# Attention and two MoE layers on one core: even heads with raw fp32 probabilities and V, bias pieces and Q's low parts on VectorE

## The chip, the core and the metric

The kernel runs on one core of a Trainium2 chip. Five engines take their instructions in order, each from its own queue: TensorE (PE; its weight loads are shown apart as PEld), VectorE (DVE), ScalarE (ACT), GpSimd (POOL) and SyncE (SP, which issues DMAs). They wait for each other through semaphores. The metric is the device time of one execution in microseconds.

## What is computed

Attention over 2 batches, 8 heads, 576 positions and 64 channels with a bias that a small network makes of the relative position, then two mixture-of-experts layers with 8 experts each. The change is in attention alone:

```python
scores = scale * np.matmul(q, k.transpose(0, 1, 3, 2))
x = (psi_rel / psi_i)[..., None]            # 576 x 576, from log1p of distance and position
h = np.maximum(x @ w1 + b1, 0.0)            # 32 hidden
bias = h @ w2                               # one column a head
scores = scores + bias.transpose(2, 0, 1)[None, :, :, :]
scores = scores - np.max(scores, axis=-1, keepdims=True)
attn = np.exp(scores)
attn = attn / (np.sum(attn, axis=-1, keepdims=True) + 1e-09)
return np.matmul(attn, v).astype(np.float32)
```

## The kernel before

Queries are cut into nine tiles `t` of 128 rows: tiles 0 to 7 are four row blocks `it` of both batches in turn, tile 8 holds the last 64 rows of both batches. A tile has 8 heads, so there are 72 pairs (t, h), walked in this order.

The bias does not depend on the batch. It is made per row block `it` in pieces of 32 keys (`NPC` is 18; the last block has 9 pieces, since its two batches share them). Each piece is one comparison on DVE (`bias_mask`, tile `mask`, L246 or L249), 16 matmuls into one PSUM bank (`bias_mm`, tile `pm`, L259) and `bias_out`: either ACT copies `pm` out (`abst`, L271) and POOL multiplies and adds (`btmp`, L272; `bias`, L273), or, with `direct`, DVE does both steps from PSUM (L267, L268). Before, only pieces 5, 9 and 13 of block 0 are direct. Block 0 is made ahead of the first head, the blocks 1 to 4 between the heads of the block before. In the heads `pm` has a single buffer, `mask` three and `btmp` two.

For a head, `s_mm` makes scores of two fp32r parts of Q (L321), `s_max` adds the bias and takes the maximum on DVE (L329), `s_exp` is the exponential on ACT with the row sum (L339), `p_turn` transposes four blocks of 128 keys on PE into PSUM (L353). `p_hi` has ACT write the transposed probabilities, times 4096, as f16 (`pth`, L359), `p_lo` has DVE write what f16 left out (`ptl`, L364), and `av` multiplies them with V in three f16 matmuls for each of the four blocks: high by high, high by low, low by high (L382). V has its f16 parts `VH` and `VL` from `v_split` (L302, L303), after its largest magnitude has been found (`v_sums`, `v_scale`). 576 is 4 x 128 + 64: the remainders of two heads at a time share a block, so a tile has a ninth product `h == H` with the remainder's V (`VRH`, `VRL`, L310, L311). `recip` (L388 to L390) and `finish` (L396) divide by the sums.

`s_mm` runs `LEAD` (3) heads ahead and `s_exp` one; `av` of a head stands two heads behind. Q is split into fp32r parts by ACT and POOL (`q_split`, L152, L153), once a tile; K by ACT and DVE (L167). The code order is a wish only: a scheduler places the instructions of attention on the engines by its own costs; the last eight steps of tile 8 stand in an order written by hand (`manual_schedule`). The MoE layers behind begin with what `finish` wrote.

The lines of `av` that count:

```python
for i, (l_, r_) in enumerate(((th, vh), (th, vl), (tl, vh))):
    nc.tensor.matmul(o.acc[ii, cs], l_[:, cc, ii], r_, start=h == 0 and cc == 0 and i == 0, stop=i == 2,
```

Of the kernel before, what the change touches and what calls it, by code (L numbers as in the profile page):

```python
# [95 lines left out]
def attention(tc, ctx, g, a, out, setup, on_tile, on_slot):  # L96
# [89 lines left out]
    vraw = prep.tile([P, BH * 4 * D], F32, name="vraw")  # L186
    for x in range(2):
        nc.sync.dma_start(vraw[:, x * 2 * VC:(x + 1) * 2 * VC], a["a_v"][:, x * 2 * VC:(x + 1) * 2 * VC])
    vrem = prep.tile([P, BH // 2, D], F32, name="vrem")
    nc.sync.dma_start(vrem, a["a_vr"].rearrange("p (t d) -> p t d", d=D))  # L190
# [89 lines left out]
    def v_sums(vm, x):  # L280

        junk = prep.tile([P, VC], F16, tag="junk", name="junk", bufs=2)
        src = vraw[:, x * VC:(x + 1) * VC] if x < 4 else vrem.rearrange("p a d -> p (a d)")
        nc.scalar.activation(junk[:, :src.shape[1]], src, AF.Abs, accum_out=vm[:, x:x + 1])

    def v_scale(vm, stage_):
        if stage_ == 0:
# [9 lines left out]
        return pow2_scales(nc, keep, vmx, "sv")  # L297

    def v_split(x):
        cs = slice(x * VC, (x + 1) * VC)  # L300
        vh = VH.rearrange("p a b d -> p (a b d)")[:, cs]
        nc.scalar.mul(vh, vraw[:, cs], sv)  # L302
        nc.vector.scalar_tensor_tensor(VL.rearrange("p a b d -> p (a b d)")[:, cs], vraw[:, cs], sv, vh, ALU.mult, ALU.subtract)  # L303

    def v_rem():
        nc.gpsimd.memset(VRH, 0.0)
        nc.gpsimd.memset(VRL, 0.0)
        for r in range(2):
            rr = slice(r * 64, r * 64 + 64)
            nc.scalar.mul(VRH[rr, :, r], vrem[rr], sv[rr])  # L310
            nc.vector.scalar_tensor_tensor(VRL[rr, :, r], vrem[rr], sv[rr], VRH[rr, :, r], ALU.mult, ALU.subtract)  # L311
# [43 lines left out]
    def p_hi(t, h, ccs=slice(0, 4)):  # L355
        o = tiles[t]
        if h not in o.av:
            o.av[h] = [late.tile([P, 4, P], F16, tag=f"pt{x}", name="pt" + x, bufs=5) for x in "hl"]
        nc.scalar.mul(o.av[h][0][:, ccs], o.pt[h][:, ccs], PSC)  # L359

    def p_lo(t, h, ccs=slice(0, 4)):
# [915 lines left out]
```

## Time and profile before

| what | value |
|---|---|
| three runs, median (lowest to highest) | 645.55 us (643.68 to 645.91) |
| profiled execution, its own time | 643.15 us |
| span of the profiled execution | 641.4 us |
| busy share PE, DVE, ACT, POOL | 85%, 73%, 62%, 50% |
| granted clock of PE, mean | 0.962 |

Attention takes the first 253 us of the span, the two MoE layers the rest. Ahead of the heads, until about 53 us, stand the bias of block 0 and the preparation of Q, K and V. A busy share of the whole span says little here, as the stretches have different limits. In the rows below times are in us from the span's start unless marked ns. Instructions of one engine overlap a little at their ends, so prices of one are read from start to start where a row of the next is given; a matmul's duration holds its whole way through the array, of which only a small part keeps the next one waiting.

### The profile page before, as it was taken

Reading aid. Unit: us, or ns where it says so; the run is one execution under the profiler, and the core shown is the slowest. Engines: PE = TensorE matmul, PEld = TensorE weight load, DVE = VectorE, ACT = ScalarE, POOL = GpSimd, SP = SyncE. Lnnn points to the kernel's source line nnn. Section 1 sums busy time; section 2 is a strip of 40 time slices with the busy share of each in tenths; the row PEclk is TensorE's granted clock in tenths of the full one; section 3 lists DMA queues with packets and bytes.
Section 4 is the critical chain, followed back from the end, with each engine's and each line's share of the span. In section 5 each row is a group of like instructions: output and inputs, shape, how many; then the busy total and the mean of one; then the engine's idle time right before and its main releaser. Section 6 shows DMA issues by size and latency. Waiting matters only on the chain. (4 is left out here: it accounts for less than half of the span.)

```text
span 641.4 us, 13184 instructions
## 1 busy us (share of the span) xinstructions
PE 546.4 (85%) x4970; PEld 461.5 (72%) x4970; DVE 466.1 (73%) x721; ACT 399.8 (62%) x667; POOL 319.4 (50%) x285
## 2 busy tenths in 40 slices
PE   2455678888888999789999999999889999999991
PEld 2444667778887888567788788777767887877771
DVE  5799999999999786887951262189768924948960
ACT  3566877888888865567842452378516736837840
POOL 3997899988877460425431141144213422434440
PEclk9777979998999999999999999999899999999997
DMA  7921654111010492788980180078755932957900
GB/s 222 326 77 34 164 136 138 49 51 28 19 35 19 85 306 69 220 264 296 330 304 29 59 276 30 30 249 292 258 165 167 330 129 84 322 171 216 336 5 8
DMA packets 47909, 101.44 MB, mean 158 GB/s; under 512 B 11780, under 2 KB 13700, under 8 KB 47536
## 3 DMA queue, kind: packets, MB, share of 16 engines
q1 hardware_dynamic: 40640, 92.12, 44.8%
q0 software_dynamic: 6272, 7.49, 3.6%
q8 instruction: 63, 1.03, 0.7%
q14 instruction: 54, 0.44, 0.2%
q10 hardware_dynamic: 880, 0.35, 0.2%
HBM read 97.47 MB, written 13.67 MB: 173 GB/s over the span
## 5 line engine op out<-in xcount | busy, mean ns | idle before, releaser
L911 DVE TENSOR_TENSOR wl<-raw,wh 128x1024 fp32r<-128x1024 f32 x125 | 156.4, 1289 | 20.8 <-ACT wh L898 15.7
L964 PE MATMUL py<-wh,hT 128*128 128x512 f32 x400 | 141.2, 404 | 0.0
L898 ACT CAST wh<-raw 128x1024 fp32r<-128x1024 f32 x110 | 113.9, 1051 | 6.5 <-ACTq L1169 2.6
L994 DVE TENSOR_TENSOR hT<-pt,hT 128x512 fp32r<-128x512 f32 x50 | 34.6, 692 | 89.0 <-ACT hT L993 88.9
L272 POOL TENSOR_TENSOR btmp<-abst,xp 128x256 f32<-128x256 f32 x78 | 80.1, 1027 | 17.1 <-ACT abst L271 16.0
L964 PEld LDWEIGHTS py<-wh,hT 128*128 128x128 f32 x400 | 75.2, 188 | 15.1
L259 PE MATMUL pm<-wmov,mask 128*128 128x64 f16 x1296 | 58.8, 204 | 29.8 <-DVE wmov L234 12.3
L964 PE MATMUL py<-wl,hT 128*128 128x512 f32 x200 | 78.2, 391 | 0.0
L259 PEld LDWEIGHTS <-mask 128*128 128x128 f16 x1296 | 53.0, 106 | 34.6 <-DVE mask L246 24.5
L273 POOL TENSOR_TENSOR bias<-abst,btmp 128x256 f32<-128x256 f32 x78 | 72.1, 925 | 5.8
L321 PE MATMUL s<-K,Q 128*128 128x288 f32 x320 | 63.3, 322 | 12.7 <-DVE mx L329 9.5
L339 ACT ACTIVATE P<-sb,mx 128x576 f32<-128x576 f32 x72 | 55.8, 776 | 24.4 <-DVE mx L329 20.3
L246 DVE TENSOR_TENSOR mask<-toep,T 128x1024 f16<-128x1024 f16 x72 | 70.3, 993 | 0.8 <-PE pm L259 0.5
L271 ACT ACTIVATE abst<-pm,swi 128x512 f32<-128x512 f32 x78 | 53.0, 685 | 20.1 <-PE pm L259 18.6
L353 PE MATMUL pt<-ident,P 128*128 128x128 f32 x324 | 54.2, 290 | 10.1 <-DVE ptl L364 5.7
L329 DVE CUSTOM_DVE_ANT_0 sb<-s,bias 128x576 f32<-128x576 f32 x72 | 53.9, 751 | 7.9 <-PE s L321 4.5
L364 DVE SCALAR_TENSOR_TENSOR ptl<-pt,pth 128x512 f16<-128x512 f32 x81 | 54.8, 680 | 5.2 <-ACT pth L359 5.0
L964 PE MATMUL ph<-wh,xh 128*128 128x512 f32 x120 | 50.1, 418 | 8.6 <-PEq L1169 7.7
L321 PEld LDWEIGHTS s<-K,Q 128*128 128x128 f32 x320 | 46.8, 194 | 14.0 <-issue 8.4
L359 ACT ACTIVATE pth<-pt 128x512 f16<-128x512 f32 x81 | 47.6, 592 | 8.6 <-PE pt L353 7.3
L993 ACT CAST hT<-pt 128x512 fp32r<-128x512 f32 x50 | 29.4, 587 | 36.4 <-PE pt L988 31.8
L1033 POOL DMA_INDIRECT y_tok<-y,si x13 | 18.0, 1382 | 67.6 <-ACT y L1025 41.1
(216 smaller groups left out, 1189.7 us busy)
## 6 DMA issues: line engine op xcount, KB each, us to landing
raw<-m_w_dram SPq DMA_DIRECT2D x64, 512.0 KB, 5.1
...
```

The lines of the kernel that those rows point to most:

```text
L246: nc.vector.tensor_tensor(m, w, T[:, i0:i0 + P].unsqueeze(1).to_broadcast([P, 8, P]), ALU.is_gt)
L259: nc.tensor.matmul(pm[:, :, :, gq * 4:gq * 4 + 4], m[:, gq], wmov[:, part], start=part == 0, stop=part == 1)
L272: nc.gpsimd.tensor_tensor(tmp, ab_[:, 0], xp, ALU.mult)
L273: nc.gpsimd.tensor_tensor(biases[it][:, :, cs], ab_[:, 1], tmp, ALU.add)
L321: nc.tensor.matmul(ps[:, half, :288], Q[:, part, h], K[:, b * H + h, half * 288:half * 288 + 288], start=i == 0, stop=i == last)
L329: nc.vector.tensor_tensor_reduce(sb.rearrange("p (t j) -> p t j", t=2), o.ps.pop(h)[:, :, :288], biases[o.it][:, h].rearrange("p (t j) -> ...
L339: nc.scalar.activation(o.Pt[hp][:, x * S:(x + 1) * S], sb, AF.Exp, bias=mx, scale=-1.0, accum_out=o.sums[:, h:h + 1])
L353: nc.tensor.transpose(pt[:, cc], src, ident)
L364: nc.vector.scalar_tensor_tensor(tl[:, ccs], o.pt.pop(h)[:, ccs], PSC, th[:, ccs], ALU.mult, ALU.subtract)
L898: eng.copy(hi, r)
L911: eng.tensor_tensor(lo, self.raw.pop((ge, j)), hi.bitcast(F32), ALU.subtract)
L964: self.nc.tensor.matmul(ps, x[a_][:, xs], w[b_][:, ws], start=first and i == 0, stop=last and i == 2)
```

## The change

- Even heads (`whole(h)`) keep V as it is (`V_`, fp32) and the transposed probabilities as fp32 (`pT`, one copy by ACT); `av` has one fp32 matmul per block in place of three f16 ones, and `p_lo` does nothing for them. Odd heads stay as they were. The remainder product also is fp32: half of its rows, of the odd heads, are scaled to fit (`VR`, `odd`). In the hand-written end two of the copies are DVE's.
- Only the odd heads' V is split: two `v_sums` and two `v_split` remain of five and four; `v_rem` goes.
- In block 0 eight pieces are direct instead of three; in the later blocks every third piece (`w[1] % 3 == 1`), 21 in all.
- Q's low parts are DVE's for all tiles but the first.
- Buffers: `pT` three; `pth` and `ptl` two each instead of five; `mx` three instead of four.

```diff
-VC = BH * 4 * D // 4
-VAT = 11, 13, 15, 17
-DIRECT = 5, 9, 13
+DIRECT = 1, 3, 5, 7, 9, 11, 13, 15
...
-    VH = keep.tile([P, BH, 4, D], F16, name="VH")
-    VL = keep.tile([P, BH, 4, D], F16, name="VL")
-    VRH = keep.tile([P, BH // 2, 2, D], F16, name="VRH")
-    VRL = keep.tile([P, BH // 2, 2, D], F16, name="VRL")
+    V_ = keep.tile([P, BH // 2, 4, D], F32, name="V")
+    VR = keep.tile([P, BH // 2, 2, D], F32, name="VR")
+    VH = keep.tile([P, BH // 2, 4, D], F16, name="VH")
+    VL = keep.tile([P, BH // 2, 4, D], F16, name="VL")
+    odd = keep.tile([P, 2], F32, name="odd")
...
-            nc.gpsimd.tensor_tensor(Q[:, 1], qr, Q[:, 0].bitcast(F32), ALU.subtract)
+            (nc.vector if t else nc.gpsimd).tensor_tensor(Q[:, 1], qr, Q[:, 0].bitcast(F32), ALU.subtract)
...
+        sv, isv = pow2_scales(nc, keep, vmx, "sv")
+        nc.vector.tensor_scalar(odd[:, 0:1], sv, PSC, None, ALU.mult)
+        nc.vector.tensor_scalar(odd[:, 1:2], isv, 1 / PSC, None, ALU.mult)
+        nc.vector.tensor_scalar(VR[64:, :, 1], VR[64:, :, 1], odd[64:, 0:1], None, ALU.mult)
+        return sv
...
-        mx = late.tile([P, 1], F32, tag="mx", name="mx", bufs=4)
+        mx = late.tile([P, 1], F32, tag="mx", name="mx", bufs=3)
...
+    def whole(h):
+        return h % 2 == 0
+
+    def p_out(t, h, eng=nc.scalar):
...
+        if whole(h):
+            o.av[h] = late.tile([P, 4, P], F32, tag="pT", name="pT", bufs=3)
+            (eng.copy if eng is nc.scalar else eng.tensor_copy)(o.av[h], o.pt.pop(h))
+        else:
+            o.av[h] = [late.tile([P, 4, P], F16, tag=f"pt{x}", name="pt" + x, bufs=2) for x in "hl"]
+            nc.scalar.mul(o.av[h][0], o.pt[h], PSC)
...
-        th, tl = o.av[h]
-        nc.vector.scalar_tensor_tensor(tl[:, ccs], o.pt.pop(h)[:, ccs], PSC, th[:, ccs], ALU.mult, ALU.subtract)
...
+        if not whole(h):
+            th, tl = o.av[h]
+            nc.vector.scalar_tensor_tensor(tl, o.pt.pop(h), PSC, th, ALU.mult, ALU.subtract)
...
+                if h == H:
+                    terms = [(pT, VR[:, b * 4 + cc].rearrange("p t d -> p (t d)"))]
+                elif whole(h):
+                    terms = [(pT, V_[:, (b * H + h) // 2, cc])]
                 else:
...
+                    vh, vl = VH[:, (b * H + h) // 2, cc], VL[:, (b * H + h) // 2, cc]
+                    terms = [(pT[0], vh), (pT[0], vl), (pT[1], vh)]
...
-            bias_out(*w)
+            bias_out(*w, w[1] % 3 == 1)
         outq = []
         p_turn(*u)
-        p_hi(*u)
+        p_out(*u)
...
-        p_hi(t, 6)
-        p_lo(t, 6)
+        p_out(t, 6, nc.vector)
...
-        p_hi(t, H)
+        p_out(t, H, nc.vector)
```

DVE at the end of the part ahead of the heads, before (`btmp` and `bias` with `pm` are the two steps of a direct piece, `sb,mx` is the first L329):

```order
L246 TENSOR_TENSOR mask<-toep,T 128x1024
L268 SCALAR_TENSOR_TENSOR bias<-pm,swi,btmp 128x8x32
L303 SCALAR_TENSOR_TENSOR VL<-vraw,svs,VH 128x1024 x3
L311 SCALAR_TENSOR_TENSOR VRL<-vrem,svs,VRH 64x8x64 x2
L303 SCALAR_TENSOR_TENSOR VL<-vraw,svs,VH 128x1024
L661 COPY enT<-pt 128x32
L329 ISA sb,mx<-s,bias 128x576
```

The same place on DVE after:

```order
L247 TENSOR_TENSOR mask<-toep,T 128x1024 x2
L268 SCALAR_TENSOR_TENSOR btmp<-pm,swi,xp 128x256
L247 TENSOR_TENSOR mask<-toep,T 128x1024
L269 SCALAR_TENSOR_TENSOR bias<-pm,swi,btmp 128x8x32
L307 SCALAR_TENSOR_TENSOR VL<-vraw,svs,VH 128x1024
L247 TENSOR_TENSOR mask<-toep,T 128x1024
L268 SCALAR_TENSOR_TENSOR btmp<-pm,swi,xp 128x256
L247 TENSOR_TENSOR mask<-toep,T 128x1024
L269 SCALAR_TENSOR_TENSOR bias<-pm,swi,btmp 128x8x32
L661 COPY enT<-pt 128x32
L247 TENSOR_TENSOR mask<-toep,T 128x1024
L325 ISA sb,mx<-s,bias 128x576
```

The splits of V that stood in a row are fewer and spread, direct pieces alternate with masks up to the first head, and two masks of block 1 (the last two here) now stand ahead of it.

DVE early in tile 1, behind `finish` of tile 0, before:

```order
L396 TENSOR_TENSOR x<-acc,rinv 128x512
L246 TENSOR_TENSOR mask<-toep,T 128x1024
L364 SCALAR_TENSOR_TENSOR ptl<-pt,pth 128x512
L329 ISA sb,mx<-s,bias 128x576
L329 ISA mx 128x1
L167 TENSOR_TENSOR K<-kraw,K 64x1152
L364 SCALAR_TENSOR_TENSOR ptl<-pt,pth 128x512
L246 TENSOR_TENSOR mask<-toep,T 128x1024
L329 ISA sb,mx<-s,bias 128x576
```

And after:

```order
L402 TENSOR_TENSOR x<-acc,rinv 128x512
L268 SCALAR_TENSOR_TENSOR btmp<-pm,swi,xp 128x256
L247 TENSOR_TENSOR mask<-toep,T 128x1024
L269 SCALAR_TENSOR_TENSOR bias<-pm,swi,btmp 128x8x32
L325 ISA sb,mx<-s,bias 128x576
L325 ISA mx 128x1
L166 TENSOR_TENSOR K<-kraw,K 64x1152
L247 TENSOR_TENSOR mask<-toep,T 128x1024
L152 TENSOR_TENSOR Q<-qraw,Q 128x1024
L368 SCALAR_TENSOR_TENSOR ptl<-pt,pth 128x512
L325 ISA sb,mx<-s,bias 128x576
```

Where each head had its `ptl`, one of two is left; a direct piece's two steps, with a mask between them, and Q's subtraction stand in the queue instead.

## Rows read from the trace of the kernel before

**Rows 1.** Busy time by stretch: from:to, length, busy time and count per engine, PE clock, DMA.

```profile
40.00:54.00 14.00, 4.06 (x45) 3.53 (x46) 13.36 (x18) 9.21 (x12) 13.45 (x10) 0.61 0.33 85
120.00:140.00 20.00, 17.54 (x313) 16.07 (x312) 20.00 (x38) 16.70 (x36) 18.93 (x19) 1.00 0.14 42
220.00:235.00 15.00, 14.86 (x187) 13.89 (x187) 12.96 (x32) 11.61 (x28) 5.81 (x4) 1.00 0.84 244
```

**Rows 2.** Timeline of POOL ahead of the heads: start, duration, instruction.

```profile
51.18 1.58 POOL L273 TENSOR_TENSOR bias<-abst,btmp 128x256 f32<-128x256 f32 x1
```

**Rows 3.** Timeline of DVE ahead of the heads; in brackets idle time and releaser.

```profile
26.48 0.48 DVE L267 SCALAR_TENSOR_TENSOR btmp<-pm,swi,xp 128x256 f32<-128x256 f32 x1 [2.90 <-POOL bias L273]
...
43.55 4.70 DVE L303 SCALAR_TENSOR_TENSOR VL<-vraw,svs,VH 128x1024 f16<-128x1024 f32 x3
48.18 2.34 DVE L311 SCALAR_TENSOR_TENSOR VRL<-vrem,svs,VRH 64x512 f16<-64x512 f32 x2
...
52.80 0.76 DVE L329 CUSTOM_DVE_ANT_0 sb<-s,bias 128x576 f32<-128x576 f32 x1 [0.51 <-POOL bias L273]
```

**Rows 4.** Groups of DVE's instructions, 54.16 to 250 us: count, busy us, mean ns, idle before.

```profile
L246 DVE TENSOR_TENSOR mask<-toep,T 128x1024 f16<-128x1024 f16 x53 | 53.8, 1023 | 0.2
L364 DVE SCALAR_TENSOR_TENSOR ptl<-pt,pth 128x512 f16<-128x512 f32 x79 | 53.5, 680 | 5.2 <-ACT pth L359 5.0
...
L167 DVE TENSOR_TENSOR K<-kraw,K 64x1152 fp32r<-64x1152 f32 x6 | 10.9, 1816 | 0.2
...
L388 DVE TENSOR_SCALAR rinv<-sums 128x8 f32<-128x8 f32 x8 | 5.8, 720 | 0.3 <-ACT P L339 0.3
```

**Rows 5.** Timeline of DVE and POOL in tile 1.

```profile
101.33 0.69 DVE L246 TENSOR_TENSOR mask<-toep,T 128x1024 f16<-128x1024 f16 x1
101.94 0.67 DVE L364 SCALAR_TENSOR_TENSOR ptl<-pt,pth 128x512 f16<-128x512 f32 x1
102.53 0.74 DVE L329 CUSTOM_DVE_ANT_0 sb<-s,bias 128x576 f32<-128x576 f32 x1
...
106.07 2.38 POOL L153 TENSOR_TENSOR Q<-qraw,Q 128x1024 fp32r<-128x1024 f32 x1
...
106.84 2.17 DVE L246 TENSOR_TENSOR mask<-toep,T 128x1024 f16<-128x1024 f16 x1
```

**Rows 6.** Line L167: shortest, median, longest ns, first and last start.

```profile
L167 DVE TENSOR_TENSOR K<-kraw,K x8: 1355/1642/3414, 20.7 to 96.6; 64x1152 fp32r<-64x1152 f32 x8
```

**Rows 7.** Timeline of DVE near attention's end.

```profile
250.22 0.16 DVE L388 TENSOR_SCALAR rinv<-sums 128x8 f32<-128x8 f32 x1
```

**Rows 8.** Timeline of PE in tile 1.

```profile
101.46 1.06 PE L692 MATMUL s<-enT,xT 128*128 128x8 f32 x8 [1.31 <-DVE mx L329]
...
103.09 0.19 PE L382 MATMUL acc<-VH,pth 128*128 128x64 f16 x1
...
103.44 0.63 PE L353 MATMUL pt<-ident,P 128*128 128x128 f32 x4
103.83 0.78 PE L321 MATMUL s<-K,Q 128*128 128x288 f32 x4
104.44 0.64 PE L259 MATMUL pm<-wmov,mask 128*128 128x64 f16 x16
```

**Rows 9.** Timeline of PE, the remainder's product and what follows.

```profile
239.18 0.22 PE L382 MATMUL acc<-VRH,pth 128*128 128x128 f16 x1
...
239.85 0.61 PE L353 MATMUL pt<-ident,P 128*128 128x128 f32 x4
```

**Rows 10.** Timeline of DVE, the last step of tiles 1 and 5.

```profile
118.56 0.68 DVE L396 TENSOR_TENSOR x<-acc,rinv 128x512 f32<-128x512 f32 x1
...
205.71 0.68 DVE L396 TENSOR_TENSOR x<-acc,rinv 128x512 f32<-128x512 f32 x1
```

**Rows 11.** Timeline of PE, scores of two heads of tile 8.

```profile
230.29 1.30 PE L321 MATMUL s<-K,Q 128*128 128x288 f32 x8
...
232.18 1.30 PE L321 MATMUL s<-K,Q 128*128 128x288 f32 x8
```

More of the change, by code (lines that the diff above doesn't have):

```diff
@@ L185, in attention @@
     k_load(0)
[L186 to L190, printed above, removed]
+    vraw = prep.tile([P, BH // 2, 4, D], F32, name="vraw")
+    for v, half in ((vraw, 1), (V_, 0)):
+        nc.sync.dma_start(v.rearrange("p a c d -> p (a c d)"), a["a_v"][:, half * BH * 2 * D:(half + 1) * BH * 2 * D])
+    nc.gpsimd.memset(VR, 0.0)
+    for r in range(2):
+        rr = slice(r * 64, r * 64 + 64)
+        nc.sync.dma_start(VR[rr, :, r], a["a_vr"][rr].rearrange("p (t d) -> p t d", d=D))
     k_load(1)
@@ L296, in v_scale, with v_split @@
         nc.vector.tensor_copy(vmx, v_scale.p[:, P:P + 1])
[L297 to L311, printed above, removed]
+        sv, isv = pow2_scales(nc, keep, vmx, "sv")
[3 more added lines that the diff above has]
+        return sv
+    def v_split(b):
+        raw = vraw[:, b * 4:b * 4 + 4].rearrange("p a c d -> p a (c d)")
+        vh, vl = (x[:, b * 4:b * 4 + 4].rearrange("p a c d -> p a (c d)") for x in (VH, VL))
+        nc.scalar.mul(vh, raw, sv)
+        nc.vector.scalar_tensor_tensor(vl, raw, sv, vh, ALU.mult, ALU.subtract)
     def s_mm(t, h):
@@ L353, in p_turn, with p_lo, av @@
             nc.tensor.transpose(pt[:, cc], src, ident)
-    def p_hi(t, h, ccs=slice(0, 4)):
+    def whole(h):
+        return h % 2 == 0
+    def p_out(t, h, eng=nc.scalar):
         o = tiles[t]
[L357 to L361, printed above, removed]
+        if whole(h):
[4 more added lines that the diff above has]
+            nc.scalar.mul(o.av[h][0], o.pt[h], PSC)
+    def p_lo(t, h):
         o = tiles[t]
-        th, tl = o.av[h]
-        nc.vector.scalar_tensor_tensor(tl[:, ccs], o.pt.pop(h)[:, ccs], PSC, th[:, ccs], ALU.mult, ALU.subtract)
-    def av(t, h, ccs=range(4)):
+        if not whole(h):
+            th, tl = o.av[h]
+            nc.vector.scalar_tensor_tensor(tl, o.pt.pop(h), PSC, th, ALU.mult, ALU.subtract)
+    def av(t, h):
         o = tiles[t]
@@ L369, in av @@
             o.acc = psA.tile([P, 512], F32, tag="acc", name="acc")
-        th, tl = o.av[h]
-        for cc in ccs:
+        pT = o.av.pop(h)
+        for cc in range(4):
             for b, _, _ in o.qs:
@@ L374, in av @@
                 pos = None if t < 8 else (0, b * 64)
-                if h < H:
-                    cs = slice(h * D, (h + 1) * D)
-                    vh, vl = VH[:, b * H + h, cc], VL[:, b * H + h, cc]
-                else:
-                    cs = slice(cc * P, (cc + 1) * P)
-                    vh, vl = (V_[:, b * 4 + cc].rearrange("p t d -> p (t d)") for V_ in (VRH, VRL))
-                for i, (l_, r_) in enumerate(((th, vh), (th, vl), (tl, vh))):
-                    nc.tensor.matmul(o.acc[ii, cs], l_[:, cc, ii], r_, start=h == 0 and cc == 0 and i == 0, stop=i == 2,
+                cs = slice(h * D, (h + 1) * D) if h < H else slice(cc * P, (cc + 1) * P)
+                if h == H:
+                    terms = [(pT, VR[:, b * 4 + cc].rearrange("p t d -> p (t d)"))]
+                elif whole(h):
+                    terms = [(pT, V_[:, (b * H + h) // 2, cc])]
+                else:
+                    vh, vl = VH[:, (b * H + h) // 2, cc], VL[:, (b * H + h) // 2, cc]
+                    terms = [(pT[0], vh), (pT[0], vl), (pT[1], vh)]
+                for i, (l_, r_) in enumerate(terms):
+                    nc.tensor.matmul(o.acc[ii, cs], l_[:, cc, ii], r_, start=h == 0 and cc == 0 and i == 0, stop=i == len(terms) - 1,
                                      tile_position=pos, skip_group_check=True)
@@ L387, in recip @@
         r = o.r = bw.tile([P, H], F32, tag="rinv", name="rinv")
-        nc.vector.tensor_scalar(r, o.sums, 1e-9, PSC, ALU.add, ALU.mult)
+        nc.vector.tensor_scalar(r, o.sums, 1e-9, None, ALU.add)
         nc.vector.reciprocal(r, r)
-        nc.vector.tensor_scalar(r, r, isv, None, ALU.mult)
+        nc.vector.tensor_scalar(r[:, 1::2], r[:, 1::2], odd[:, 1:2], None, ALU.mult)
     def finish(t):
@@ L403, in attention @@
     rot = (psM, "pm"), (psT, "pt"), (psT, "pt"), (psS, "s"), (psS, "s")
-    vm = prep.tile([P, 6], F32, name="vm")
+    vm = prep.tile([P, 4], F32, name="vm")
     for x in range(NPC + 2):
```

44 lines of the change are left out of this document (19 added, 25 removed).

## The prediction

> **What bounds the kernel now.** I read the stretches first [rows 1]. In the middle of attention VectorE (DVE) is busy 20.00 of 20 us while TensorE (PE) shows 17.54, and PE's figure is inflated, since its instructions overlap. So DVE sets the pace of the heads. Towards the end of attention (220 to 235 us) the masks are gone and PE is busy 14.86 of 15: there PE sets it. Ahead of the heads GpSimd (POOL) does, 13.45 of 14 us in 40 to 54 [rows 1]: its bias additions follow each other to 52.76 [rows 2], and the first subtraction of scores on DVE (L329, at 52.80) waits its last 0.51 us for them [rows 3]. The MoE layers behind take their input from attention's end and none of their code changes, so I let them move with it.
>
> DVE's own rows then say what its time is made of [rows 4]. A mask takes 1023 ns in the mean, but 0.69 us where nothing disturbs it; where POOL subtracts the low parts of Q (2.38 us from 106.07) the mask that starts at 106.84 takes 2.17 us and ends with POOL [rows 5]. The two engines shut each other out. The evictions `ptl` that read PSUM are not touched: 680 ns in the mean, 0.67 us beside POOL's work too [rows 4, 5]. Nor is a bias step from PSUM: 0.48 us [rows 3]. The Trainium skill's SBUF — State Buffer (Who interferes with whom) says the same of a DVE instruction with two SBUF inputs: it and a GpSimd instruction that reads SBUF hold one port for the whole instruction. By that rule the Q subtraction on DVE stays exposed to POOL, with which the price of K's subtraction below agrees.
>
> **Ahead of the heads** (to the first L329). POOL loses 5 of its 15 pieces, a third of its chain, and is no longer last. With it go DVE's waits for POOL, 2.90 and 0.51 us: -3.4. DVE drops two of four `VL` splits (three take 4.70, so 1.57 each): -3.1, and both `VRL` (2.34): -2.3 [rows 3]. It takes five more pieces of two steps, each 0.48 less the 0.07 by which DVE instructions overlap, 0.82 a piece: +4.1 [rows 3]. Scaling half of VR and two one-column products: no such row; between 0.3 and the 1.17 of one VRL step, I take 0.8 in all. Masks: 14 follow here, each some 0.2 over its floor by the heads' rows below once Q's collisions are left out; with a third of POOL's pieces gone I take a third of that: -1.0. Sum -4.9. New is that DVE, which takes its queue in order, waits for PE's 16 matmuls of its own pieces; behind it stand masks, for which PE waits in turn. The schedule puts a mask between, so I take 0.6 for all eight, between 0 and 4. **-4.3** (bounds -6 and -1). The two masks of the next block that now stand ahead of the first L329 are only moved.
>
> **The heads as far as DVE sets the pace** (54 to 215). Prices from start to start, as instructions overlap by about 0.07.
> - `ptl` of even heads and remainders goes: 45 of 81. By the lead of three heads 33 lie ahead of 215 and 12 behind. 0.60 each (101.94 to 102.53) [rows 5]: -19.8. The copy of the transposed probabilities on ScalarE stays an instruction of the same 128x512, priced at nothing new.
> - 21 pieces (six of 18 in each of three blocks, three of nine in the last) from PSUM, 0.82 each: +17.2. ScalarE and POOL lose them; neither sets the pace there.
> - Q's low parts, nine on DVE, 128x1024 from two SBUF tiles. The nearest row is K's subtraction, 64x1152: 1355 ns at least, 1642 at the median [rows 6]. 1355 x 1024/1152 less the overlap is 1.15 (upper bound 1.45 by the median): +10.4, and 0.3 each for POOL's bias steps beside them: +2.7.
> - The collisions with POOL's Q go. Eight DVE instructions stand beside one: a K subtraction with 3414 for 1355 ns [rows 6], 2.06, and seven masks, three of them as the 2.17 in place of 0.69 [rows 5], 4.4. The four others, not shown, are 0.4 to 1.9 over the floor in the same view, 4.0: -10.5, of which 8.4 on masks.
> - What POOL's bias steps cost DVE: masks 53.8 less 53 x 0.69, 17.2; K's 10.9 less 6 x 1.36, 2.7; L388 5.8 less 8 x 0.16, 4.5 [rows 4, 5, 7]. Less the 10.5 that is 14.0. Of POOL's pieces a third goes: -4.7 (bounds 0 and -9).
>
> DVE: -19.8 + 17.2 + 10.4 + 2.7 - 10.5 - 4.7 = -4.7. So the two moves to DVE eat nearly all that the dropped evictions free; what is left is contention.
>
> **What PE pays.** An odd head's product is 12 f16 matmuls in 0.35 us (103.09 to 103.44) [rows 8], 29 ns each. An even head's is 4 fp32 matmuls. The one true fp32 product before is the router's (L692): 4 of them are 8 instruction pairs in 1.06 us, the last some 0.27 long, so some 112 ns from one to the next though only 8 columns stream [rows 8]: its weights set that. 64 columns fit under it: 8 pairs, 0.90, +0.55 a head. Lower bound 0.35 (+0); upper, if two passes of the stream at f16's 29 ns came on top of the weights: 170 a pair, 1.36, +1.01. The remainder now takes 0.67 (239.18 to 239.85) [rows 9], then 0.90: +0.23. The Trainium skill's FP8 and Floating Point Precision (TensorE Precision Notes) speaks of four passes for true fp32: 4 x 4 x 64 columns against 12 x 64 now, a third more stream, which would be 0.12 a head in place of 0.55; the tail would come out at -0.3, nothing would be handed back below, and the sum would be -9.3. The router's row disagrees, its 8 columns cost 112, so I stay with the row.
>
> PE per tile of 8 heads before: transposes 0.39, scores 0.61 (both from 103.44 to 104.44), product 0.35, masks 16 x 0.029 for seven heads of eight, 0.41 [rows 8], 1.76 x 8 = 14.1; remainder 0.39 + 0.67, transposed x 0.4, router 0.9: 16.5. With 4 x 0.55 + 0.23 it is 18.9. A tile's period is (205.71 - 118.56)/4 = 21.8 [rows 10], by DVE's sum 0.7 less, 21.1. PE fits, with 90% instead of 76%. Two engines this full wait for each other now and then: I hand back 1.0. **-3.7** (bounds -10 and +2).
>
> **The tail** (215 to 253). Where PE sets the pace, two heads follow at 1.89 (230.29 to 232.18) [rows 11], so an even head adds its whole 0.55: five and one remainder, +3.0. In the last tile the same product has half-width weights, and ScalarE and the hand-over from ScalarE to DVE to PE set the pace; even heads lose a step of 0.6 there while their product grows by as much. I take -1.0. **+2.0** (bounds 0 and +6).
>
> **Sum.** -4.3 - 3.7 + 2.0 = -6.0. The profiled execution took 643.15 (span 641.4), so 637.2; the three runs shown have a median 2.4 above it, 645.55, which gives **639.5**.
>
> **Rivals.**
> 1. *PE becomes the bound* (slower). If a pair costs 170 and the remainder's, with 128 columns, 112 + 2 x 56 = 224 (1.79, +1.12), a tile of PE's is 16.5 + 4 x 1.01 + 1.12 = 21.7, with 3% for gaps 22.3, over the 21.8 of now: five tiles +2.5, the first two, where DVE has far more to do, -1.0; the tail 5 x 1.01 + 1.12 + 1.0 = +7.2; ahead of the heads -4.3. Together +4.4: **650.0**. It decides from about 155 a pair. For it: PE waits for every weight load in the router's row. Against: the score matmuls hide loads of the same width.
> 2. *DVE waits for its own pieces.* In the heads of before, DVE never queued behind PE's bias matmuls. PE's bias PSUM in the heads is a single buffer, held over two DVE steps now. 0.4 us at each of 21 pieces is +8.4: **647.9**, no change that can be told. Against: a mask or L329 stands between in the schedule.
> 3. *More contention goes.* POOL would be busy about half of the heads' time instead of 18.93 of 20 us [rows 1]; if two thirds of the 14.0 went and the 1.0 and 0.6 of new waits stayed away: -4.7 - 1.0 - 0.6, **633.2**. For it: a mask that starts first is at its floor [rows 5], and a POOL with pauses is first less often. Against: the bias steps that stay are as long.
>
> **Chances.** The sum 0.47, rival 1 0.16, rival 2 0.17, rival 3 0.20. The range goes from under rival 3 to over rival 2, 631.5 to 649.0; it leaves out more than half of rival 1 and the far ends of the others. A measurement of this kernel can tell 0.5%, 3.2 us. Faster by more: nearly all of the sum's case and rival 3, 0.62. Within: rival 2, the rest of the sum's and a part of rival 1, 0.25. Slower: 0.13.
>
> **What would show it.** First L329 near 48.5 instead of 52.8, with no wait for POOL before it. No mask over 1.3 us from there on, a mean near 0.85. Q's subtraction on DVE 1.2 to 1.7 us. `acc<-V,pT` in pairs 112 ns apart (170 is rival 1). DVE still over 95% in the middle, PE busier; if DVE shows waits for PE pm before the bias steps, over 5 us in all, rival 2. A tile's period of 21.0 to 21.3. The step most likely to fail is the 1.0 handed back for two full engines: a PE clock that falls, or a schedule that makes the heads wait in order, would cost more than that.

## The result and the profile after

| | before | after |
|---|---|---|
| median of 4 runs each (lowest to highest) | 644.66 us (643.68 to 645.91) | 635.57 us (634.96 to 638.97) |
| ratio, 95% interval | | 0.987 [0.983, 0.991] |
| span of the profiled execution | 641.4 us | 633.7 us |
| mean granted clock of TensorE | 0.962 | 0.967 |

The kernel became 1.3% faster. To see where, I cut the span at four instructions that both traces have: the first score subtraction on DVE (L329 before, L325 after), that of head 16 (the first head of tile 2, whose bias is block 1), that of head 56 (the first of tile 7), and the end of the last `x` (L396 before, L402 after). For the three stretches between them, busy time by engine; columns as in [rows 1]. Of the kernel before:

```profile
52.80:106.15 53.35, 40.05 (x616) 36.58 (x617) 51.45 (x78) 43.02 (x79) 46.02 (x40) 0.90 0.45 115
106.15:214.15 108.00, 93.55 (x1603) 86.33 (x1602) 102.89 (x192) 89.64 (x186) 92.22 (x98) 0.98 0.14 43
214.15:253.73 39.58, 37.60 (x602) 34.08 (x598) 32.11 (x74) 26.85 (x62) 13.84 (x8) 1.00 0.61 179
```

Of the changed kernel:

```profile
48.00:97.52 49.52, 41.62 (x567) 37.92 (x568) 46.34 (x84) 38.14 (x71) 22.92 (x24) 0.97 0.49 136
97.52:204.70 107.18, 101.85 (x1520) 96.21 (x1518) 97.38 (x203) 83.55 (x173) 55.70 (x62) 1.00 0.14 38
204.70:245.03 40.33, 40.30 (x531) 38.08 (x526) 26.93 (x65) 25.83 (x60) 11.76 (x7) 1.00 0.59 176
```

I call the stretches A (to the first subtraction), B (to head 16), C (to head 56), D (to the last `x`) and "behind". A became 4.8 us shorter, B 3.8, C 0.8; D became 0.8 longer and the part behind 1.1: together the span is 7.6 us shorter. In C DVE gave up 5.5 us of busy time and the stretch became only 0.8 shorter: PE went from 87% to 95% busy, DVE from 95% to 91%. The rows that answer to [rows 1] say the same:

```profile
40.00:54.00 14.00, 10.34 (x119) 9.81 (x117) 9.66 (x21) 6.94 (x13) 8.11 (x8) 0.78 0.25 68
120.00:140.00 20.00, 19.98 (x308) 19.27 (x305) 18.28 (x38) 15.56 (x32) 10.52 (x13) 1.00 0.26 68
220.00:235.00 15.00, 15.00 (x168) 14.54 (x166) 9.94 (x23) 9.53 (x23) 10.25 (x6) 1.00 0.76 278
```

DVE's groups from 48.00 to 204.70 us, to be held against [rows 4]:

```profile
L247 DVE TENSOR_TENSOR mask<-toep,T 128x1024 f16<-128x1024 f16 x52 | 41.6, 804 | 1.5 <-PE pm L260 1.2
L368 DVE SCALAR_TENSOR_TENSOR ptl<-pt,pth 128x512 f16<-128x512 f32 x26 | 17.6, 675 | 0.1
L152 DVE TENSOR_TENSOR Q<-qraw,Q 128x1024 fp32r<-128x1024 f32 x8 | 10.8, 1349 | 0.0
L268 DVE SCALAR_TENSOR_TENSOR btmp<-pm,swi,xp 128x256 f32<-128x256 f32 x21 | 9.9, 474 | 2.3 <-PE pm L260 2.0 <-POOL bias L274 0.2
L166 DVE TENSOR_TENSOR K<-kraw,K 64x1152 fp32r<-64x1152 f32 x6 | 8.5, 1423 | 0.2
L396 DVE TENSOR_SCALAR rinv<-rinv,odd 128x4 f32<-128x4 f32 x6 | 2.2, 359 | 0.0
L394 DVE TENSOR_SCALAR rinv<-sums 128x8 f32<-128x8 f32 x6 | 2.0, 341 | 0.0
```

and of before, 52.80 to 214.15 us, the three that [rows 4] don't have over this stretch:

```profile
L364 DVE SCALAR_TENSOR_TENSOR ptl<-pt,pth 128x512 f16<-128x512 f32 x59 | 40.0, 678 | 0.4 <-ACT pth L359 0.2
L388 DVE TENSOR_SCALAR rinv<-sums 128x8 f32<-128x8 f32 x6 | 4.7, 787 | 0.0
L390 DVE TENSOR_SCALAR rinv<-rinv,svi 128x8 f32<-128x8 f32 x6 | 4.0, 667 | 0.0
```

Masks went from 1023 to 804 ns, K's subtraction from 1816 to 1423, the two small `rinv` steps from 787 and 667 to 341 and 359. PE's rows in tile 1: an even head's product, and what follows it:

```profile
70.25 1.08 PE L388 MATMUL acc<-V,pT 128*128 128x64 f32 x8
71.41 0.64 PE L260 MATMUL pm<-wmov,mask 128*128 128x64 f16 x16
```

Eight pairs in 1.08 us, as the router's in [rows 8]: 112 ns from one start to the next.

The prediction measures a tile's period from the last step of tile 1 to that of tile 5 [rows 10]. The same two steps after:

```profile
106.46 0.67 DVE L402 TENSOR_TENSOR x<-acc,rinv 128x512 f32<-128x512 f32 x1
...
196.29 0.68 DVE L402 TENSOR_TENSOR x<-acc,rinv 128x512 f32<-128x512 f32 x1
```

That is 22.5 us a tile against 21.8 before. So tiles 2 to 5 became 2.7 us slower together, and the gain inside the heads was made ahead of them: from the first subtraction to the last step of tile 1 it is 58.5 us against 65.8.

### The profile page after: what moved, and what is told of

Its sections match the earlier page's. It is cut to its first block, busy times and chain, and to the rows that moved or that the text cites. A ratio compares the mean times of both kernels' runs of the same rounds, so it can differ in the third digit from the quotient of the medians.

```text
span 633.7 us, 12729 instructions
## 1 busy us (share of the span) xinstructions
PE 559.8 (88%) x4770; PEld 477.5 (75%) x4770; DVE 449.0 (71%) x738; ACT 379.0 (60%) x629; POOL 241.5 (38%) x223
## 5 line engine op out<-in xcount | busy, mean ns | idle before, releaser
L273 POOL TENSOR_TENSOR btmp<-abst,xp 128x256 f32<-128x256 f32 x52 | 47.9, 920 | 84.0 <-ACT abst L272 81.9
L325 DVE CUSTOM_DVE_ANT_0 sb<-s,bias 128x576 f32<-128x576 f32 x72 | 53.4, 747 | 15.9 <-PE s L317 9.1
L247 DVE TENSOR_TENSOR mask<-toep,T 128x1024 f16<-128x1024 f16 x72 | 56.6, 792 | 1.5 <-PE pm L260 1.2
L964 PE MATMUL ph<-wh,xh 128*128 128x512 f32 x120 | 50.6, 421 | 7.8 <-PEq L1169 7.0
L272 ACT ACTIVATE abst<-pm,swi 128x512 f32<-128x512 f32 x52 | 35.7, 686 | 28.2 <-PE pm L260 28.0
L274 POOL TENSOR_TENSOR bias<-abst,btmp 128x256 f32<-128x256 f32 x52 | 50.0, 962 | 4.1
L964 PE MATMUL ph<-wh,xl 128*128 128x512 f32 x120 | 47.8, 398 | 1.4 <-issue 1.4
L964 PE MATMUL ph<-wl,xh 128*128 128x512 f32 x120 | 47.5, 396 | 0.0
```

Of the source, the lines that this page charges most:

```text
L247: nc.vector.tensor_tensor(m, w, T[:, i0:i0 + P].unsqueeze(1).to_broadcast([P, 8, P]), ALU.is_gt)
L272: nc.scalar.mul(ab_, pm, isw)
L273: nc.gpsimd.tensor_tensor(tmp, ab_[:, 0], xp, ALU.mult)
L274: nc.gpsimd.tensor_tensor(biases[it][:, :, cs], ab_[:, 1], tmp, ALU.add)
L325: nc.vector.tensor_tensor_reduce(sb.rearrange("p (t j) -> p t j", t=2), o.ps.pop(h)[:, :, :288], biases[o.it][:, h].rearrange("p (t j) -> ...
L964: self.nc.tensor.matmul(ps, x[a_][:, xs], w[b_][:, ws], start=first and i == 0, stop=last and i == 2)
```

## The experiments

Each kernel was run 5 to 12 times beside the kernel before on the same chip, whose median was 645.07, 645.44 and 644.73 us in the three groups of runs. The letters are those of the stretches above; each is from one profiled execution. "vs before" is (ratio - 1) x 645. Differences against "after" are taken by these ratios, since the groups were run beside different executions of before; by the bare medians, which some expectations quote, e1 stands 10.4 and e3 8.9 us above "after".

| kernel | A | B | C | D | behind | median us | ratio [95%] | vs before |
|---|---|---|---|---|---|---|---|---|
| before | 52.8 | 53.4 | 108.0 | 39.6 | 387.6 | 644.66 | | |
| after | 48.0 | 49.5 | 107.2 | 40.3 | 388.7 | 635.57 | 0.987 [0.983, 0.991] | -8.4 |
| e1_q_on_pool | 49.4 | 57.8 | 107.3 | 40.3 | 389.3 | 645.94 | 0.999 [0.997, 1.002] | -0.6 |
| e2_no_third | 47.9 | 49.2 | 105.6 | 40.4 | 387.1 | 631.02 | 0.978 [0.976, 0.980] | -14.2 |
| e3_three_first | 51.3 | 55.1 | 106.9 | 40.4 | 387.9 | 644.47 | 0.999 [0.998, 1.000] | -0.6 |
| e4_all_f16 | 47.8 | 53.2 | 104.4 | 42.8 | 425.8 | 676.32 | 1.048 [1.046, 1.050] | |
| b1_q_dve | 52.8 | 51.4 | 106.5 | 44.2 | 392.4 | 647.44 | 1.003 [1.001, 1.005] | +1.9 |
| b2_eight_first | 50.8 | 52.2 | 108.2 | 40.1 | 388.2 | 640.95 | 0.993 [0.991, 0.995] | -4.5 |
| b3_all_but_v | 49.1 | 56.5 | 107.0 | 40.5 | 387.0 | 642.38 | 0.997 [0.994, 0.999] | -2.3 |
| e5_one_pass | 48.1 | 49.9 | 98.5 | 37.1 | 429.8 | 664.29 | 1.029 [1.027, 1.032] | |
| e6_no_low | 47.9 | 54.6 | 104.6 | 39.7 | 387.9 | 635.94 | 0.985 [0.981, 0.989] | -9.8 |
| e7_third_in_one | 47.7 | 50.3 | 102.3 | 40.4 | 389.8 | 634.37 | 0.982 [0.978, 0.987] | -11.4 |
| e8_ten_first | 46.5 | 50.6 | 102.8 | 40.3 | 392.6 | 632.57 | 0.979 [0.976, 0.983] | -13.3 |
| e9_ten_mix | 47.1 | 49.7 | 102.3 | 40.2 | 387.5 | 628.90 | 0.976 [0.971, 0.980] | -15.7 |

In e4 and e5 the even heads multiply with the odd heads' V; other values reach the router and the part behind takes some 40 us more, so only A to D of them are read. Elsewhere the part behind differs by up to 5.6 us though its code is the same, so one profile can't place a difference of that size in it.

**e1: Q's low parts back on GpSimd.**

```diff
-(nc.vector if t else nc.gpsimd).tensor_tensor(Q[:, 1], qr, ...)
+nc.gpsimd.tensor_tensor(Q[:, 1], qr, ...)
```

> The changed kernel with one part undone: Q's low parts are GpSimd's again for all tiles. Theory (the sum of the prediction): on VectorE nine subtractions of 1.335 us go (-12.0) and some eight collisions with GpSimd's 2.4 us come back (+10.5), so the time stays within 2 us of the changed kernel: ratio to the kernel before 0.984 to 0.990. Rival: it is the end of these collisions that the change lives on; then at least 4 us come back: 0.993 or more.

The whole gain is gone, +7.8 us against after by the ratios, and B lost 8.3 of it. The page of the stretch:

```profile
49.45:107.29 57.84, 45.30 (x597) 42.40 (x598) 51.29 (x86) 39.85 (x73) 30.34 (x27) 0.88 0.49 135
```

DVE is not full there, 51.29 of 57.84 us. So it isn't a matter of DVE's sum. In tile 1 the trace shows, on POOL, DVE and PE:

```profile
78.63 3.21 POOL L152 TENSOR_TENSOR Q<-qraw,Q 128x1024 fp32r<-128x1024 f32 x1 [2.12 <-ACT Q L151]
```

```profile
79.63 2.77 DVE L247 TENSOR_TENSOR mask<-toep,T 128x1024 f16<-128x1024 f16 x1
...
86.46 0.68 DVE L402 TENSOR_TENSOR x<-acc,rinv 128x512 f32<-128x512 f32 x1
```

```profile
87.19 1.97 PE L388 MATMUL acc<-V,pT 128*128 128x64 f32 x8 [5.55 <-DVE x L402]
```

and the stretches around it:

```profile
83.00:88.00 5.00, 0.81 (x4) 0.81 (x5) 5.00 (x10) 1.70 (x5) 2.46 (x3) 0.74 0.18 52
88.00:93.00 5.00, 5.00 (x55) 4.94 (x54) 4.16 (x5) 2.92 (x5) 4.04 (x2) 0.58 0.48 157
```

The mask that stands beside POOL's subtraction takes 2.77 us for 0.69. `x` is behind it in DVE's queue, PE's next product needs the PSUM that `x` reads, and PE stands still for 5.55 us. The collision itself is 2.1 of these; the rest is what else stands ahead of `x`. The scheduler changed that order with the edit: here a mask and a bias step come between the last subtraction of scores and `x`, in the changed kernel nothing does. Then the granted clock falls to 0.58 (of 5 us most at 1.2 instead of 2.4 GHz), and the eight pairs take 1.97 us instead of 1.08. So this trace shows the collision, a wait of PE behind it, and PE's slower clock after the wait; how much of the loss is the new order's was not tested. Over this kernel's runs the clock and the time go together: in eleven of the twelve (without the longest) mean clocks from 0.945 to 0.974 go with spans from 647.1 to 639.0 us, by a straight fit 2.2 us less for each 0.01 (correlation -0.81). The kernel before shows no such link (-0.10 over 29 runs), nor does e3 (-0.15), so this is no price that holds for every kernel here.

The kernel before has the same picture with K in the mask's place. POOL, DVE, PE, and the two stretches:

```profile
78.98 2.35 POOL L153 TENSOR_TENSOR Q<-qraw,Q 128x1024 fp32r<-128x1024 f32 x1
```

```profile
79.14 3.41 DVE L167 TENSOR_TENSOR K<-kraw,K 64x1152 fp32r<-64x1152 f32 x1
```

```profile
82.60 1.33 PE L321 MATMUL s<-K,Q 128*128 128x288 f32 x8 [2.15 <-DVE K L167]
```

```profile
78.00:83.00 5.00, 2.52 (x51) 2.19 (x50) 4.94 (x5) 4.63 (x9) 5.00 (x3) 1.00 0.40 109
83.00:88.00 5.00, 4.20 (x57) 3.90 (x55) 5.00 (x10) 2.04 (x4) 4.76 (x6) 0.60 0.83 188
```

In the changed kernel K's subtraction at 79.70 takes 1.35 and PE waits 0.84 for it, and the same two stretches keep the full clock:

```profile
78.00:83.00 5.00, 4.07 (x53) 3.41 (x53) 4.94 (x12) 4.69 (x10) 1.62 (x2) 1.00 0.99 297
83.00:88.00 5.00, 3.55 (x64) 3.41 (x63) 4.97 (x10) 3.70 (x8) 2.05 (x3) 1.00 0.43 154
```

**e2: no third pieces in the heads.**

```diff
-bias_out(*w, w[1] % 3 == 1)
+bias_out(*w)
```

> The changed kernel with one part undone: between the heads no bias piece is VectorE's any more, ScalarE and GpSimd make all of them; block 0 keeps its eight. Theory 1 (VectorE still sets the pace of the heads): 21 x 0.82 = 17 us less on VectorE, some 5 us of collisions more: 8 to 12 us faster than the changed kernel, ratio 0.97. Theory 2 (TensorE sets the pace of the middle tiles by now): only the first two tiles and TensorE's 6 us of waits for VectorE's second step can gain: 0 to 4 us faster, ratio 0.981 to 0.987. Theory 3 (the moved pieces pay because GpSimd is away from VectorE's masks): slower, over 0.990.

5.8 us faster than the changed kernel by the ratios, and the two intervals don't meet: this part of the change is a loss. That is between the two forecasts.

**e3: three pieces ahead of the heads instead of eight.**

```diff
-DIRECT = 1, 3, 5, 7, 9, 11, 13, 15
+DIRECT = 5, 9, 13
```

> The changed kernel with one part undone: ahead of the heads pieces 5, 9 and 13 are VectorE's, as before, instead of eight. Theory: GpSimd's chain is last again there, the first subtraction of scores moves back from 48.0 towards 52 us, and all behind it moves along: 3 to 4.5 us slower than the changed kernel, ratio 0.992 to 0.995. Rival: the 4.8 us came from the dropped splits of V; then it stays at 0.987 and the first subtraction at 48 to 49.

More than either theory: +7.8 us, 3.3 in A and 5.6 in B. That A's pieces act on B was not foreseen; PE's clock is 0.90 in its B against 0.97, but what starts that is open.

**e4: all even heads in f16 parts**, four buffers for them, products with the odd heads' V.

```diff
-return h % 2 == 0
+return h == H
```

> The changed kernel with one part undone: all eight heads of a tile use f16 parts again (the remainder product stays fp32; even heads read the odd heads' V, so the result is not theirs), with four buffers for each part. VectorE has 36 evictions of 0.60 us more (+21.6), TensorE 36 x 0.55 us less (-20). Theory 1 (VectorE sets the pace): 10 to 18 us slower than the changed kernel, ratio 1.003 to 1.015. Theory 2 (TensorE sets the pace of the middle and the end): faster than the changed kernel, ratio 0.975. If both are equally full: 0 to 6 us slower.

To the end of attention 248.2 us against 245.0: 3.2 slower, B +3.6, C -2.8, D +2.5. In all that is the case of both equally full. With the f16 products C is shorter, though DVE has the low parts of all heads in it. That spoke against DVE as what paces C.

**b1: only Q's low parts moved**, in the kernel before (the line of e1).

> The kernel before, with one part of the change alone: from the second tile on Q's low parts are made by VectorE instead of GpSimd. Putting them back to GpSimd in the changed kernel cost 10.4 us. VectorE of before was busy for 97% of the middle tiles, and the nine subtractions are 11 to 12 us of work for it. Theory 1 (what GpSimd's fp32 subtraction costs is the VectorE operation that runs beside it, a mask of 2 to 2.6 us in place of 0.69, and the mask stands on the chain that makes block 1's bias, which has to be complete before head 16): the gain is made ahead of head 16 and is 2 to 6 us, ratio 0.990 to 0.997; tiles 2 to 8 get no shorter. Theory 2 (VectorE is full, so its own 11 us use up the 10 us of collisions): ratio 0.997 to 1.003. Theory 3 (the part only pays together with the relief of the even heads, as VectorE has no room for it): slower, ratio over 1.003.

**b2: only eight pieces first**, in the kernel before (the line of e3).

> The kernel before, with one part of the change alone: eight pieces of block 0's bias instead of three are subtracted by VectorE straight from PSUM ahead of the heads. In the changed kernel three instead of eight cost 8.9 us: 3.3 ahead of the first head and 5.6 between it and head 16. Theory 1 (the pieces ahead of the heads are a chain of their own, the same in both kernels): the first score subtraction comes 3 to 4 us earlier, the rest stays: ratio 0.993 to 0.996. Theory 2 (GpSimd, freed of five pieces, comes sooner to block 1's pieces, which have to be complete before head 16, and this counts in both kernels): 6 to 9 us, ratio 0.986 to 0.991.

Alone, Q on DVE costs 1.9 us, where the same step is worth 7.8 in the changed kernel. By the time that is theory 2, at the edge of theory 3, but the profiled execution doesn't bear out their reason. DVE is full in its C (104.25 of 106.53 us), and yet B is 2.0 and C 1.5 shorter, so up to head 56 the step pays here too; D is 4.6 and the part behind 4.8 longer. In D a small step of the router on DVE meets POOL's preparation of the MoE weights, PE waits 2.15 us for it, and its clock falls:

```profile
232.55 1.98 DVE L742 TENSOR_TENSOR oh<-cm,ch 128x56 f16<-128x56 f32 x1
```

```profile
234.58 0.20 PE L747 MATMUL pr<-oh,trih 128*128 128x56 f16 x1 [2.15 <-DVE oh L742]
```

```profile
230.00:235.00 5.00, 2.74 (x34) 2.29 (x32) 4.93 (x8) 1.95 (x4) 4.92 (x4) 0.96 0.93 354
235.00:240.00 5.00, 3.81 (x27) 3.67 (x28) 3.84 (x8) 1.35 (x3) 2.83 (x2) 0.50 0.05 20
```

In the kernel before the same step takes 0.97 us. Whether b1's other executions lose their time there is not known. b2's 4.5 us lie near theory 1: 2.0 in A, where 3 to 4 were expected, and 1.2 in B.

**b3: all but V**, so the kernel before with Q, the eight pieces and the third pieces.

> The kernel before with all parts of the change but the even heads' fp32 V: eight pieces first, every third piece by VectorE in the heads, Q's low parts on VectorE. So VectorE has the changed kernel's work and the low parts of all heads besides (44 operations of 0.68 us, 30 us), and TensorE has the f16 products of before. Theory 1 (VectorE and TensorE take turns in setting the pace, so that what the even heads save VectorE is worth more than the 12 us of TensorE time it costs): 3 to 8 us slower than the changed kernel, ratio 0.990 to 1.000, the loss within the heads. Theory 2 (TensorE's fp32 pairs cost what VectorE saves): as fast as the changed kernel, ratio 0.984 to 0.989.

2.3 us faster than before, 6.1 slower than after: theory 1's number. But nearly all of it is in B (56.5 against 49.5) and 1.1 in A; C and D are alike (107.0 and 40.5 against 107.2 and 40.3). Its B:

```profile
49.08:105.59 56.51, 42.35 (x614) 38.43 (x614) 55.40 (x94) 36.93 (x70) 26.40 (x25) 0.86 0.39 110
```

DVE is busy 55.40 of 56.51 us: in B DVE paces, and the dropped evictions of even heads pay there (PE's clock is lower too, 0.86 against 0.97). From head 16 on they pay nothing; e5 shows why.

**e5: one f16 pass for even heads**, the low parts left out.

```diff
-o.av[h] = late.tile([P, 4, P], F32, tag="pT", name="pT", bufs=3)
+o.av[h] = late.tile([P, 4, P], F32 if h == H else F16, ...)
...
-terms = [(pT, V_[:, (b * H + h) // 2, cc])]
+terms = [(pT, VH[:, (b * H + h) // 2, cc])]
```

> The changed kernel, but the even heads' product for the four blocks is one f16 matmul a block with the odd heads' high part of V; the low parts are left out, so the values of the even heads are wrong. TensorE loses the fp32 pairs (8 matmul records of 112 ns a head become 4), VectorE's work stays the changed kernel's. From head 16 to the end of attention all six kernels so far took 146.0 to 147.6 us. Theory 1 (from tile 2 on TensorE sets the pace in the changed kernel: 95% busy, 20.0 of 20 us in places): this stretch shortens by 4 to 10 us, to 138 to 143 us. Theory 2 (VectorE, at 93%, is as full and takes over at once): 0 to 3 us, 144 to 147 us. Theory 3 (something outside both engines, such as a transfer, fixes it): no change within 0.5 us. The routing after attention may differ with the wrong values, so only the stretch of attention is to be read.

Head 16 to the end of attention took 135.6 us, 11.9 less; B is unchanged. Its C:

```profile
98.02:196.55 98.53, 91.44 (x1449) 83.33 (x1448) 96.68 (x202) 80.63 (x172) 56.43 (x60) 1.00 0.13 39
```

Theory 1, and more than it forecast: with PE's work cut, DVE takes over at 98% busy and 98.5 us. So DVE's queue can be done in 98.5 us, and most of the changed kernel's 107.2 is PE's doing.

**e6: no low parts of the odd heads' probabilities.**

```diff
-nc.vector.scalar_tensor_tensor(tl, o.pt.pop(h), PSC, th, ALU.mult, ALU.subtract)
...
-terms = [(pT[0], vh), (pT[0], vl), (pT[1], vh)]
+terms = [(pT[0], vh), (pT[0], vl), (pT[0], vl)]
```

> The changed kernel without the low parts of the odd heads' probabilities: VectorE loses 36 subtractions of 0.68 us (24.5 us, 7 of them ahead of head 16); TensorE keeps three f16 matmuls a block, the third reading the high part of P and the low part of V, so the result lacks a term. Theory 1 (VectorE paces tiles 0 and 1, TensorE alone paces from head 16 on, as one pass for the even heads took 11.9 us off that stretch): first subtraction to head 16 shortens by 2 to 5 us (eight such operations more cost 7.0 there), head 16 to the end of attention stays at 146 to 148 us; about 630 to 634 us. Theory 2 (both engines pace by turns after head 16 too): that stretch shortens by 3 to 8 us; about 623 to 629 us.

B and C of it:

```profile
47.85:102.49 54.64, 46.32 (x565) 42.67 (x566) 46.69 (x80) 39.22 (x72) 23.19 (x25) 0.83 0.49 133
102.49:207.12 104.63, 100.84 (x1527) 95.50 (x1525) 85.57 (x179) 82.87 (x172) 52.13 (x62) 1.00 0.12 34
```

In C DVE is left with 82% and the stretch is only 2.6 us shorter, PE at 96%: PE is the pacer, DVE's queue costs it a little. In all, from head 16 on, 3.1 us: the lowest edge of theory 2, and theory 1's "no change" is not right either. B went against both theories: 5.1 us longer with less work. With the low parts away, DVE took Q's subtraction, a `rinv` step and a mask ahead of a score subtraction; PE waited for the probabilities behind it, and its clock fell. PE, and the stretches:

```profile
79.92 0.66 PE L349 MATMUL pt<-ident,P 128*128 128x128 f32 x4 [2.34 <-ACT P L335]
```

```profile
78.00:83.00 5.00, 2.11 (x22) 1.71 (x23) 4.94 (x11) 3.20 (x7) 0.87 (x1) 0.76 1.02 266
83.00:88.00 5.00, 4.49 (x42) 4.01 (x42) 4.09 (x8) 2.86 (x5) 3.81 (x4) 0.50 0.25 91
```

As in before, e1 and b1, PE's clock falls after PE has waited. As in e1, the order that the scheduler chose is another than in the changed kernel.

**e7: third pieces in block 1 only.**

```diff
-bias_out(*w, w[1] % 3 == 1)
+bias_out(*w, w[0] == 1 and w[1] % 3 == 1)
```

> The changed kernel with the third pieces on VectorE in block 1 only; those of blocks 2 to 4 go by ScalarE and GpSimd. Without any such piece in the heads the kernel took 631.0 us, with all of them 635.6 us. Theory 1 (in block 1 they relieve GpSimd, on which head 16 waits, and pay; the later ones only fill VectorE): 627 to 631 us. Theory 2 (they cost in both): between the two, 631 to 635 us, with head 16 no earlier than 97.0 us.

Theory 2 by the median, between e2 and after, though the interval meets both. The profile shows the place of what the later pieces cost, C:

```profile
97.96:200.22 102.26, 99.01 (x1520) 95.46 (x1518) 90.18 (x172) 90.69 (x188) 84.00 (x92) 1.00 0.14 40
```

4.9 us less than after, at 97% of PE. But e2 and e8, which have no third pieces in C either, took 105.6 and 102.8 there, so 1.6 to 4.9 us less than after. They part in tile 2 alone, the first of C's five (25.2, 22.1 and 22.4 us in e2, e7 and e8; in e2 at a lower clock); the other four take 80.2 to 80.5 us in all three, and 88.3 in the changed kernel, whose tile 2 took 18.9. Tile 2 of e2:

```profile
97.01:122.17 25.16, 23.34 (x349) 22.62 (x346) 22.21 (x40) 21.55 (x44) 18.85 (x19) 0.93 0.33 96
```

In C of the changed kernel PE waits for DVE's second bias step, four times:

```profile
PE pm L260 <- DVE bias L269: 2.5, 4, 0.9
```

In e7's C it waits for ScalarE's copy in its place:

```profile
PE pm L260 <- ACT abst L272: 1.4, 4, 0.4
```

All of PE's waits there differ by 1.7 us (4.9 and 3.2). Another 2.8 show as longer busy time of PE for the same 1520 matmuls, and what lengthens it is not shown.

**e8: ten pieces first, no third pieces.**

```diff
-DIRECT = 1, 3, 5, 7, 9, 11, 13, 15
+DIRECT = 1, 3, 5, 7, 9, 11, 13, 15, 16, 17
```

> The changed kernel without third pieces in the heads, and with two more pieces ahead of the heads (the last two) by VectorE. There, VectorE stood idle for 3.0 us before the first score subtraction, and GpSimd's last two pairs for block 0 took from 44.34 to 47.82 us. Theory 1 (the end of GpSimd's last pair releases the first head): the first subtraction comes 1.2 to 1.8 us earlier, at 46.1 to 46.7 us, and all after it as much: about 629 to 630 us, ratio 0.975 to 0.977. Theory 2 (TensorE or the scores hold the first head too): at 47.3 us or later, ratio 0.978.

The first score subtraction came at 46.48 with no wait before it, 1.4 us earlier, as theory 1 had it:

```profile
46.48 0.74 DVE L325 CUSTOM_DVE_ANT_0 sb<-s,bias 128x576 f32<-128x576 f32 x1
```

The total doesn't show it: 0.979 against e2's 0.978, intervals over each other. Nor does head 16, which comes at 97.05 against e2's 97.01: B took 1.4 us longer, so what came after did not move along, as theory 1 had it. The profiled execution also had 392.6 us behind attention against e2's 387.1.

**e9: ten pieces first, fp32 V for heads 0 and 4 only.**

```diff
-return h % 2 == 0
+return h % 4 == 0
```

(with V's layout, its scale and the buffers to match)

> As the one with ten pieces first, but only heads 0 and 4 use fp32 V and probabilities; heads 2 and 6 use f16 parts. Per tile TensorE loses two fp32 heads' extra (0.55 us each, 1.1 us) and VectorE gains two operations of 0.68 us (1.4 us); without third pieces TensorE was busy for 84.8 and VectorE for 77.4 of 88.0 us in tiles 2 to 5, so 21.2 and 19.4 us a tile of 22.0 become 20.1 and 20.7. Theory 1 (from head 16 on TensorE paces, and the two loads now balance): head 16 to the end of attention 140 to 144 us instead of 146.0; ahead of head 16 four operations more on VectorE, 2 to 4 us more; in all 625 to 630 us. Theory 2 (VectorE is near enough to full, at 88%, that it takes over at once): 630 to 635 us.

The best of all, 628.90 us, its interval below that of after, and by the numbers theory 1: from head 16 to the end of attention 142.5 us. C:

```profile
96.87:199.13 102.26, 96.10 (x1562) 91.55 (x1560) 94.42 (x183) 91.14 (x188) 84.11 (x92) 1.00 0.13 37
```

The loads are balanced, PE 94% and DVE 92%, but e8's stretch from head 16 on was already at 143.2, not the 146.0 of e2 that the expectation started from. C is only 0.6 shorter than e8's, and B 0.8 shorter where 2 to 4 longer was expected. So balance gave little. The intervals of e8 and e9 meet, so that the mix itself gains is not shown.

## Why the prediction was right, and where it was not

The time was forecast as 639.5 and is 635.57, faster as forecast and inside the range. By its parts: ahead of the heads -4.3, measured -4.8; the heads to 215 us -3.7, measured -4.6 (B and C); the tail +2.0, measured +0.8; behind it 0, measured +1.1. Every part is near, but inside the heads two terms were far off and cancelled, and ahead of them another path than the one summed gave the size. That these two parts came out near is luck.

- **Ahead of the heads.** The size was right, the mechanism only in part. The -4.3 was a sum over DVE, and POOL was to be no longer last. POOL still is, and its shorter chain sets the -4.8; DVE stood idle for 3.0 us before it:

```profile
48.00 0.76 DVE L325 CUSTOM_DVE_ANT_0 sb<-s,bias 128x576 f32<-128x576 f32 x1 [3.01 <-POOL bias L274]
```

  So DVE finished earlier than forecast, and e8 starts the heads 1.4 us sooner by giving DVE the last two pieces too.
- **DVE's own work.** 33 `ptl` fewer (59 to 26), 21 pieces at 474 and 471 ns, eight Q subtractions at 1349 ns (forecast 1.2 to 1.7): as priced.
- **Contention** was mis-sized. Q's collisions -10.5 and POOL's steps -4.7 make -15.2, and +2.7 for Q's subtractions beside POOL makes -12.5. Measured between the first subtraction and head 56: masks 53.8 to 41.6, one of 0.7 less; K 10.9 to 8.5; `rinv` 4.7 + 4.0 to 2.0 + 2.2; the other groups 1.3: -11.5 - 2.4 - 4.5 - 1.3 = -19.7 (a little of it because the second `rinv` step now has half its columns), against which Q's eight stand 1.1 over their shortest, 1212 ns. So it came to -18.6, 6 us more than forecast. The -19.7 is rival 3's size (10.5 + two thirds of 14.0 = 19.8). The forecast counted one of the two `rinv` steps and let a third of the rest go. The Trainium skill's SBUF — State Buffer (Who interferes with whom), by which Q's subtraction on DVE stays exposed to POOL, agrees with its 1212 to 1747 ns here. The price is small, 1349 in the mean, while Q on POOL made a mask 2.77 us long.
- **The 1.0 handed back for two full engines** is the step that failed, as the prediction feared. DVE's busy time in B and C fell by 10.6 us (154.34 to 143.72) and the time by 4.6, so 6.0 were handed back. A tile's period was to be 21.1, paced by DVE. By the prediction's own steps it is (196.29 - 106.46)/4 = 22.5, longer than the 21.8 of before (C as a whole gives 107.18/5 = 21.4 against 21.6). It is paced mostly by PE (e5, e6), DVE at 91% and not over 95%. Up to the last step of tile 1 DVE gave up 8.8 us and the time fell by 7.3; from there to head 56 DVE gave up 1.8 and the time rose by 2.6.
- **PE's price** was right: 112 ns a pair. Rival 1's price of 170 was wrong; that PE becomes the bound from head 16 on is nevertheless what happened, at the lower price. The forecast let PE fit because its sum came to 18.9 a tile. That was too low: even e7, where PE's waits in C come to 3.2 us, takes 102.26/5 = 20.5. What fills the difference is not shown. The Trainium skill's FP8 and Floating Point Precision (TensorE Precision Notes) has four passes; priced by the stream alone, 0.47 a head by the estimate in the prediction, they don't give the time. The row shows 0.9.
- **Rival 2** came in part and in mirror image: DVE waits for PE's pieces only 2.0 us in three waits, but PE waits 2.5 us for the PSUM that DVE holds over two steps, and e2 shows the third pieces as a loss (-5.8 us without them). The prediction's own terms said so: +17.2 on DVE, of which POOL's steps, -4.7, gave back little.
- **Q on DVE** was worth +2.6 by the sum (+10.4 + 2.7 - 10.5). In the kernel before it is +1.9 (b1), but not for the sum's reason: the heads up to 56 gained 3.5 us and the loss came behind them. In the changed kernel it is worth -7.8 (e1), nearly all in B. There the collision's price is also PE's wait and clock, and in part the order that the scheduler chose. A sum over one engine has no place for that.
- **The tail.** PE is busy 40.30 of 40.33 us, as forecast, and yet it grew by only 0.8; the low bound of 0 was nearer than the 2.0 taken.

Open: why five pieces ahead of the heads act on B (e3), how much of B's differences is the clock's, how much the waits' own and how much the scheduler's new order, which every edit brings with it, and what moves the part behind attention. The smaller buffers, the fp32 remainder product and the hand-written end were not tested by themselves.
